# Attention scores in rounds of three tiles with three PSUM buffers, and one shared PSUM bank for all other matrix work

## The chip, the cores and the metric

The kernel runs on one core of a Trainium2 chip. The metric is the time of one execution on the device in microseconds (us); lower is better. The core has a matrix engine (PE, TensorE) that writes only to PSUM, a memory of eight banks with 512 fp32 columns on 128 partitions each; a vector engine (DVE, VectorE); an engine for functions such as the exponential (ACT, ScalarE); GpSimd (POOL) and SyncE (SP), which here issue DMA transfers.

## The reference

Two independent layers, whose outputs are concatenated. `A` is a long convolution over 2048 positions for 576 channels: a kernel K is generated from a state-space model, and y = irfft(rfft(u) * rfft(K)) + u * Dskip. `B` is attention with one shared key and value head:

```python
q = (x @ wq).reshape(B, S, H, Dh).transpose(0, 2, 1, 3)   # 32 heads of 18, S = 2048
k, v = x @ wk, x @ wv                                     # one head of 18
scores = einsum("bhqd,bkd->bhqk", q, k) * Dh ** -0.5
o = einsum("bhqk,bkd->bhqd", softmax(scores), v)
out_b = o.transpose(0, 2, 1, 3).reshape(B, S, 576) @ wo
```

Everything is fp32.

## The kernel before

**Attention** (class `Attention`). The 2048 queries are cut into four chunks `c` of 512, the heads into eight groups `g` of four, the keys into 16 blocks `kb` of 128. That gives 512 steps (line 587). In a step, `scores` (L350) is called for two pairs of heads: two matmuls with 55 rows each fill the two banks of one score tile `s` (128 keys x 2 heads x 512 queries), and one ScalarE instruction (L362) writes the exponentials to a tile `P` in SBUF. The 55 rows hold q and k split into a high and a low part, and a bound on the scores, so no row maximum is needed. The product (L628) of the step before then multiplies four heads of `P` by v, in four 32-column strips of the array, and adds up over the 16 blocks in the bank `ops`; a column of ones in v gives the softmax denominator. At the 16th block VectorE copies `ops` out (`gather`, L365) and SP stores it.

**Other matrix work**, called filler here, is put between scores and product. `qproj` (L271) makes the queries of seven heads and 512 positions, as two halves of 256 columns with five chunks of matmuls each; `queries` (L288) then splits them with three reads of the whole bank on VectorE, distributes the rows by DMAs of POOL, and makes the bound with a small matmul `up`. `outproj` and `outproj_part` (L408, L432) make the output `op` in pieces of 288 columns. The class `Conv` makes the convolution in twelve blocks of 48 channels: tables on VectorE and ScalarE, `kgen` (L887, tile `kg`), two forward transforms per block (`transform`, L930, tiles `lu`, `hu`, `lk`, `hk`), long VectorE arithmetic, and an inverse transform `iy` (L1018). Every one of them is a group of matmuls into a bank, followed by VectorE reading the bank out.

**PSUM** (lines 168 to 171): two score tiles of two banks, one bank `ops`, two banks `q` which q, op and up take in turn, one bank `m` for the convolution. Eight banks in all.

**The order** of PE, ScalarE and VectorE is that of the program text; PE works it off in that order. `main` (L578) decides it when the program is written out, with a model of the three engines' clocks (`Clock`). Generators (`Stream`) give their work piece by piece and say what the next piece needs: "p" is PE work that may start at a time `ready`, "v" is VectorE work, and a flag `holds` says that a group of matmuls is open. In each step, after the two scores, filler is taken as long as a credit lasts (about 0.56 us of PE time a step, from `TOTAL` and `LAST`), then comes the product. `q_free` and `Conv.free` are the model's times at which a bank is read out.

Of the kernel before, what the change touches and what calls it, by code (L numbers as in the profile page):

```python
# [31 lines left out]


RATE = 1.75
AHEAD = 0.8
# [17 lines left out]
class Clock:  # L53
# [6 lines left out]
    def __init__(self):  # L60
        self.t = self.v = self.a = 0.0
        self.work = 0.0
        self.s = [0.0, 0.0]
# [4 lines left out]
    def act(self, cost, after=0.0):  # L68
        self.a = max(self.a, after) + cost
        return self.a  # L70

# [36 lines left out]
class Stream:  # L108
# [18 lines left out]
    def go(self, step, credit):  # L127

        k = self.k
        if not self.live or self.kind == "b" or self.kind == "p" and (credit <= 0 or k.t < self.ready):  # L130
            return False
        if self.kind == "v" and (k.t < self.ready or k.v > k.t + self.ahead):
            return False
        if self.kind == "w":
            if self.asked == step:
                return False
            self.asked = step
        self.advance()
        return True
# [10 lines left out]
class Attention:  # L150
# [7 lines left out]
    def __init__(self, tc, ctx, aps, clock):  # L158
# [7 lines left out]
        self.pp = pool("a_p", 4)  # L166
        self.dr = pool("a_dr", 4, space=bass.MemoryType.DRAM)
        self.ps_s = pool("ps_s", 2, space=PSUM)
        self.ps_o = pool("ps_o", 1, space=PSUM)
        self.ps_q = pool("ps_q", 2, space=PSUM)  # L170
        self.ps_m = pool("ps_m", 1, space=PSUM)
# [9 lines left out]
    def setup(self, tp, conv):  # L181
# [8 lines left out]
        self.sel = cp.tile([P, 138], F32, name="sel_sb")  # L190
# [27 lines left out]
        nc.scalar.dma_start(self.sel, a["sel"])  # L218
# [6 lines left out]
        self.outs, self.step, self.due, self.q_free, self.scaled = [], 0, 1 << 30, [0.0, 0.0], {}  # L225
# [3 lines left out]
        kps = self.ps_q.tile([P, CT], F32, tag="q", name="kps")  # L229
        self.qps = self.ps_q.tile([P, CT], F32, tag="q", name="q0_0")  # L230
        pv = self.ps_m.tile([P, CT], F32, tag="m", name="vps")
        for k in range(5):
            for ps, j in ((kps, 0), (None, 0), (pv, 32)):
                if ps is None:
                    matmul4(nc, self.qps, self.wq[0][:, k, :], x0[:, k, :], start=(k == 0), stop=(k == 4))
                    continue
                for c in range(NCH):
                    nc.tensor.matmul(ps[32 * c:32 * c + 32, :], wkv[:, k, j:j + 32], xr[:, k, c - 1, :] if c else x0[:, k, :],
                                     start=(k == 0), stop=(k == 4), tile_position=(0, 32 * c))
        nc.scalar.activation(kh, kps, AF.Copy)  # L240
        V.tensor_reduce(km[:, 4:5], kps, axis=AX.X, op=ALU.max, apply_absolute_value=True)
        V.tensor_scalar(km[:, 0:4], self.sel[:, 134:138], km[:, 4:5], None, op0=ALU.mult)
# [12 lines left out]
        pk = self.ps_q.tile([P, 4], F32, tag="q", name="kmx")  # L255
        nc.tensor.matmul(pk[:126, :], self.sel[:, 8:134], km[:, 0:4], start=True, stop=True)
# [4 lines left out]
        vp = self.ps_m.tile([P, 4, P], F32, tag="m", name="vp")  # L261
# [9 lines left out]
    def qproj(self, c, m, xt):  # L271

        nc, V, K = self.nc, self.V, self.k
        m0, mn = MT[m]
        self.q_left = 10
        yield "p", max(self.q_free[0], K.t), False
        ps = self.ps_q.tile([P, CT], F32, tag="q", name=f"q{c}_{m}")
        for f in range(2):
            sl = slice(f * 256, f * 256 + 256)
            for k in range(5):  # L280
                matmul4(nc, ps[:, sl], self.wq[m][:, k, :], xt[:, k, sl], start=(k == 0), stop=(k == 4))
                K.pe(0.43)
                self.q_left -= 1
                if (f, k) != (1, 4):
                    yield "p", 0.0, True
        yield from self.queries(c, m, ps)

    def queries(self, c, m, ps):  # L288
# [3 lines left out]
        K.v = max(K.v, K.t)  # L292
        qh = self.p2.tile([P, CT], F32R, tag="qh", name=f"qh{c}_{m}", bufs=1)
        ql = self.p2.tile([P, CT], F32R, tag="ql", name=f"ql{c}_{m}", bufs=1)
        ab = self.p2.tile([P, 1], F32, tag="ab", name=f"ab{c}_{m}")
        if (c, m) == (0, 0):
            nc.scalar.activation(qh[:mn, :], ps[:mn, :], AF.Copy)
        else:
            V.tensor_copy(qh[:mn, :], ps[:mn, :])
            V.tensor_tensor(ql[:mn, :], ps[:mn, :], qh[:mn, :].bitcast(F32), op=ALU.subtract)  # L300
        V.tensor_reduce(ab[:mn, :], ps[:mn, :], axis=AX.X, op=ALU.max, apply_absolute_value=True)
        if (c, m) == (0, 0):
            V.tensor_tensor(ql[:mn, :], ps[:mn, :], qh[:mn, :].bitcast(F32), op=ALU.subtract)
# [22 lines left out]
        yield "p", max(K.v + 0.4, self.q_free[0]), False  # L326

        up = self.ps_q.tile([P, 8], F32, tag="q", name=f"up{c}_{m}")
# [5 lines left out]
        self.q_free = self.q_free[1:] + [K.v + 0.3]  # L334
# [15 lines left out]
    def scores(self, c, pr, kb):  # L350

        nc = self.nc
# [5 lines left out]
        K = self.k  # L358
        K.pe(0.335, K.s[pr % 2])
        K.s[pr % 2] = K.act(0.925, K.t + 0.27) + 0.1  # L360
# [4 lines left out]
    def gather(self, c, g, o_ps):  # L365
        nc = self.nc
        o_sb = self.p2.tile([P, CT], F32, tag="o", name=f"o{c}_{g}")
        self.k.v = max(self.k.v, self.k.t)
        self.V.tensor_copy(o_sb, o_ps)
        nc.sync.dma_start(self.od[c][g * P:(g + 1) * P, :], o_sb)  # L370
# [37 lines left out]
    def outproj(self, c):  # L408
        nc, V, K = self.nc, self.V, self.k
        o = self.oT  # L410
        self.o_left += 40
        yield "p", max(self.scaled[4], self.q_free[0]), False
        for t in range(4):
            ob = self.p1.tile([P, D], F32, tag="ob", name=f"ob{c}_{t}", bufs=2)
            for nh in range(2):
                ps = self.ps_q.tile([P, 288], F32, tag="q", name=f"op{c}_{t}_{nh}")
                for m, (m0, mn) in enumerate(MT):
                    matmul4(nc, ps, o[:mn, m, t * P:(t + 1) * P], self.wo[:mn, m, nh * 288:(nh + 1) * 288], start=(m == 0), stop=(m == 4))
                    K.pe(0.5)
# [4 lines left out]
                V.tensor_copy(ob[:, nh * 288:(nh + 1) * 288], ps)  # L424
                self.q_free = self.q_free[1:] + [K.v + 0.3]
                if nh == 0:
                    yield "p", self.q_free[0], False
            nc.sync.dma_start(self.a["outb"][c * CT + t * P:c * CT + (t + 1) * P, :], ob)
            if t < 3:
                yield "p", self.q_free[0], False  # L430

    def outproj_part(self, c, ms, part):  # L432
# [3 lines left out]
        self.o_left += 8 * len(ms)  # L436
        for t in range(4):
            for nh in range(2):
                yield "p", max(self.scaled[ms[-1]], self.q_free[0]), False
                ps = self.ps_q.tile([P, 288], F32, tag="q", name=f"op{c}_{t}_{nh}_{ms[0]}")  # L440
                cs = slice(nh * 288, (nh + 1) * 288)
                for m in ms:
                    matmul4(nc, ps, o[:126, m, t * P:(t + 1) * P], self.wo[:126, m, cs], start=(m == ms[0]), stop=(m == ms[-1]))
                    K.pe(0.5)
# [8 lines left out]
                self.q_free = self.q_free[1:] + [K.v + 0.3]  # L453

    def finish(self, c, part, o_ps, w4, b4):
# [3 lines left out]
        o_sb = self.p2.tile([P, CT], F32, tag="o", name="o_last")  # L459
        rc = self.p2.tile([P, CT], F32, tag="o", name="rc_last")  # L460
        half = [slice(f * 256, f * 256 + 256) for f in range(2)]
        cols = [slice(nh * 288, nh * 288 + 288) for nh in range(2)]
        bc = self.ps_m.tile([P, CT], F32, tag="m", name="bc")
# [14 lines left out]
        def invert(f):  # L478
            V.reciprocal(rc[:, half[f]], rc[:, half[f]])
            nc.tensor.matmul(bc[:, half[f]], b4, rc[:, half[f]], start=True, stop=True)  # L480

        def scale(f):
            V.tensor_tensor(o_sb[:, half[f]], o_sb[:, half[f]], bc[:, half[f]], op=ALU.mult)
        for nh in range(2):
            begin(0, nh, self.ps_q.tile([P, CT], F32, tag="q", name=f"fin0_{nh}"))
        for t in (1, 2):
# [18 lines left out]
        begin(3, 1, self.ps_q.tile([P, CT], F32, tag="q", name="fin3_1"))  # L505
# [6 lines left out]
    def side(self):  # L512
# [3 lines left out]
        yield from self.queries(0, 0, self.qps)  # L516
# [23 lines left out]
    def prepare(self):  # L540

        nc = self.nc
        while True:
# [11 lines left out]
            if ms[0] == 3:  # L555
                self.w4 = self.p1.tile([P, D], F32, tag="ob", name="w4", bufs=2)
# [21 lines left out]
    def main(self, conv, flag):  # L578
# [4 lines left out]
        K.t = K.v = K.a = conv.free = 0.0  # L583
        side.ready, self.q_free = 0.0, [0.0, 0.0]
        for st in conv.streams:
            st.ready = 0.0
        steps = [(c, g, kb) for c in range(NCH) for g in range(8) for kb in range(16)]
        prev, o_ps, credit, filled = None, None, 0.0, 0.0

        prep = Stream(self.prepare(), K, 99.0)  # L590

        def drain():
            while self.todo or self.busy or self.outs:
                if self.todo or self.busy:
                    prep.advance()
                if self.outs:
                    side.advance()
        for i, at in enumerate(steps + [None]):
            cur = None
            if at is not None:  # L600
                self.step = i
                c, g, kb = at
                if (g, kb) == (0, 0):
                    self.od[c] = self.dr.tile([8 * P, CT], F32, tag="od", name=f"od{c}")
                cur = [self.scores(c, 2 * g, kb), self.scores(c, 2 * g + 1, kb)]
                ready = K.act(0.0)
                credit = min(credit + min(max((TOTAL - filled) / max(LAST - i, 20), 0.45), 0.58 if i < 384 else 0.68), 0.75)
                nxt = (c, 2 * g + 3) if g < 7 else (c + 1, 1)
                more = True
                while more:  # L610
                    more, t = False, K.t

                    idle = max(K.s[0] - K.t - 0.96, K.s[1] - K.t - 1.3) - 0.15
# [568 lines left out]
```

## Time and profile before

| | |
|---|---|
| median of 3 runs | 1288.39 us (1286.58 to 1291.62) |
| the profiled execution | 1288.89 us, span of its instructions 1287.0 us |
| PE matmul records | 1223.3 us, 95% of the span |
| ScalarE | 1064.3 us, 83% |
| VectorE | 991.5 us, 77% |
| idle time of ScalarE ahead of exponentials, ended by PE's scores | 179.3 us |
| mean granted PE clock | 0.989 |

The span runs from the first to the last instruction. A group in the profile is a source line, an engine, an operation and its tiles, written out<-in; x is the count. "PEld" is the loading of weights into PE, which overlaps matmuls. In a timeline each row has its start, its duration, and in brackets how long the engine had been idle and what ended that. Rows of one kind that follow one another are merged with their count; an fp32 matmul of the program is two records (two passes), a score matmul is one.

### The profile page before, as it was taken

To read this page: it belongs to the slowest core of one execution; us is meant where nothing else is said; L and a number is where in the kernel's file an instruction comes from. 1 tells how busy PE (TensorE), PEld (TensorE's weight loads), DVE (VectorE), ACT (ScalarE), POOL (GpSimd) and SP (SyncE) were. 2 spreads that over 40 slices of the span, in tenths; PEclk is the share of its full clock that TensorE was granted. 3 is DMA by queue.
4 is the path that set the end of the run, shared out by engine and by line. 5 is a ranking of instruction groups with operands and counts; after the bars stand their busy time and mean duration, and the time that the engine had idled before them with its cause. 6 is when DMAs were issued, how large, how long until landed. Compare 5 with 4: busy or idle time off the path is not lost.

```text
span 1287.0 us, 32922 instructions
## 1 busy us (share of the span) xinstructions
PE 1223.3 (95%) x13762; PEld 472.4 (37%) x13762; DVE 991.5 (77%) x1612; ACT 1064.3 (83%) x1101; POOL 227.8 (18%) x450
## 2 busy tenths in 40 slices
PE   5999999899999999999999999999899999899997
PEld 1333343243334344343334334334233334334332
DVE  4778878878878968978977976976977987786842
ACT  2689989888988888888888888888988888788884
POOL 3342102203110110231312110221302120110000
PEclk9899999899999999999999999999999999899999
DMA  7621022121120112021122011312103112021011
GB/s 224 174 70 35 17 67 65 30 75 47 53 75 23 42 58 76 25 82 51 36 75 71 29 51 42 99 33 76 31 27 107 29 40 66 13 59 64 26 39 39
DMA packets 56779, 75.35 MB, mean 59 GB/s; under 512 B 19393, under 2 KB 30017, under 8 KB 56113
## 3 DMA queue, kind: packets, MB, share of 16 engines
q1 hardware_dynamic: 35784, 58.22, 13.8%
q0 software_dynamic: 20288, 14.39, 5.1%
q8 instruction: 110, 1.80, 0.6%
q10 hardware_dynamic: 552, 0.58, 0.1%
q14 instruction: 45, 0.36, 0.1%
HBM read 35.28 MB, written 22.54 MB: 45 GB/s over the span
## 4 chain that ended last, share of the span: by engine, by line
PE 67%; issue 12%; DVE 12%; ACT 6%; POOL 1%; DMA 1%; SPq 0%; DVEq 0%; ACTq 0%; POOLq 0%
PE ops L628 24%; PE s L357 21%; ACT P L362 6%; PE op L147 5%; PE q L147 4%; PE kg L898 3%; PE iy L147 2%; DVE ks L86 2%; DVE acc L86 2%; PE lu L147 1%; PE hu L147 1%; PE hk L147 1%; PE lk L147 1%; POOL aug L321 1%; DVE f L86 1%
## 5 line engine op out<-in xcount | busy, mean ns | idle before, releaser
L362 ACT ACTIVATE P<-s 128x1024 f32<-128x1024 f32 x1024 | 985.7, 1023 | 188.7 <-PE s L357 179.3
L628 PE MATMUL ops<-P,v_sb 128*32 128x512 f32 x4096 | 548.8, 601 | 4.9 <-DVE o L90 4.6
L357 PE MATMUL s<-aug,kaug 55*128 55x512 f32 x2048 | 432.5, 475 | 38.2 <-ACT P L362 35.1
L357 PEld LDWEIGHTS s<-aug,kaug 55*128 55x128 f32 x2048 | 186.2, 185 | 543.0 <-ACT P L362 523.8
L321 POOL DMA_DIRECT2D aug<-qh x252 | 127.0, 520 | 769.0 <-DVE qh L90 394.3
L628 PEld LDWEIGHTS ops<-P,v_sb 128*32 128x32 f32 x4096 | 116.9, 110 | 90.8 <-issue 35.1
L147 PE MATMUL q<-x,wq_sb 128*32 128x256 f32 (+2 forms) x1480 | 105.9, 396 | 0.0
L147 PE MATMUL op<-wo_sb,oT 126*32 126x288 f32 (+1 forms) x1152 | 94.8, 414 | 0.0
L90 DVE COPY ksb<-kg 128x192 f32<-128x192 f32 x48 | 17.6, 366 | 83.3 <-PE kg L898 83.3
L321 POOL DMA_DIRECT2D aug<-ql x128 | 65.0, 523 | 8.4 <-issue 5.4
L86 DVE TENSOR_TENSOR tab<-tab,tt 128x576 f32<-128x576 f32 (+1 forms) x72 | 59.2, 822 | 1.8
L147 PEld LDWEIGHTS q<-x,wq_sb 128*32 128x32 f32 (+1 forms) x1480 | 42.5, 109 | 47.6 <-issue 26.3
L86 DVE TENSOR_TENSOR tab<-tab 128x576 f32<-128x576 f32 (+1 forms) x72 | 59.0, 819 | 1.0
L347 POOL DMA_DIRECT2D aug<-sh x61 | 35.2, 586 | 134.0 <-DVE sh L94 133.7
L86 DVE TENSOR_TENSOR tab<-sum,r 128x576 f32<-128x576 f32 (+1 forms) x72 | 58.9, 818 | 0.0
L86 DVE TENSOR_TENSOR tt<-f,sum 128x576 f32<-128x576 f32 (+1 forms) x72 | 58.8, 817 | 0.0
L86 DVE TENSOR_TENSOR tab<-r,dif 128x576 f32<-128x576 f32 (+1 forms) x72 | 58.8, 817 | 0.0
L86 DVE TENSOR_TENSOR sck<-lk,sck 128x384 f32<-128x384 f32 x48 | 24.5, 553 | 31.7 <-PE lk L147 31.7
L86 DVE TENSOR_TENSOR acc<-acc,pt 128x1728 f32<-128x1728 f32 (+2 forms) x36 | 48.7, 1353 | 0.2
L86 DVE TENSOR_TENSOR pt<-us,ks 128x1728 f32<-128x1728 f32 (+2 forms) x36 | 48.7, 1352 | 0.1
L86 DVE TENSOR_TENSOR u<-u,iy 128x384 f32<-128x384 f32 x24 | 13.3, 554 | 38.3 <-PE iy L147 38.3
L898 PE MATMUL kg<-tab 128*32 128x64 f32 x2304 | 42.1, 221 | 0.4 <-DVE tab L86 0.4
(118 smaller groups left out, 1003.7 us busy)
## 6 DMA issues: line engine op xcount, KB each, us to landing
aug<-qh POOLq DMA_DIRECT2D x252, 36.0 KB, 1.9
od<-o SPq DMA_DIRECT2D x31, 256.0 KB
aug<-ql POOLq DMA_DIRECT2D x128, 36.0 KB, 2.0
u<-u SPq DMA_DIRECT2D x12, 384.0 KB
kd<-ksb SPq DMA_DIRECT2D x12, 384.0 KB
kt<-kd SPq DMA_DIRECT2D x48, 96.0 KB
outa<-u SPq DMA_DIRECT2D x12, 384.0 KB
oT<-od SPq DMA_DIRECT2D x16, 252.0 KB
```

The lines of the kernel that those rows point to most:

```text
L86: return self.v.tensor_tensor(out, *a, **k)
L90: return self.v.tensor_copy(out, *a, **k)
L147: nc.tensor.matmul(ps[j:e], w[:, j:e], x, start=start, stop=stop, tile_position=(0, j))
L321: q.dma_start(t[b:b + 18, :], src[r:r + 18, :])
L347: nc.gpsimd.dma_start(self.aug[(c, h // 2)][54:119:64, :], sh)
L357: nc.tensor.matmul(ps[:, j, :], self.kaug[r, kb * P:(kb + 1) * P], t[r, :], start=True, stop=True)
L362: nc.scalar.activation(pt, ps, AF.Exp, scale=SCALE)
L628: nc.tensor.matmul(o_ps[32 * j:32 * j + 32, :], self.v[:, pk, :], pts[j // 2][:, j % 2, :], start=(pk == 0), stop=(pk == 15), tile_positio ...
L898: nc.tensor.matmul(ps[32 * g:32 * g + 32, d, :], t[:, :32], t[:, 32:], start=(j == 0), stop=(j == 1), tile_position=(0, 32 * g))
```

## The change

- There are three score tiles (`NS` = 3), six banks. A round computes three of them, that is three pairs of heads, one after the other, then the three exponentials; products of the rounds before follow, each when its two `P` tiles are there. There are six `P` buffers instead of four.
- One bank `fb` of two halves of 256 columns takes all other matrix work, in turn (`half`). The model keeps two times `fill` at which the halves are read out; a group may start at `fill[0]`, the older one.
- To fit a half, groups get smaller. A transform makes four groups of 192 columns where it made two of 384, each with its own reads by VectorE; `iy` likewise; `op` is made in three pieces of 192 columns instead of two of 288; each half of `q` is read out by itself.
- Only one group of matmuls may be open at a time (`lock`, `holder`).
- `o` and `ob` have one buffer instead of two. The setup uses score buffers, `ops` and `fb` for its own matmuls, and loads `sel` in two parts.

The core of the diff, lines left out:

```diff
+NS = 3
+NP = 6
...
+    def filled(self, least=0.0):
+        self.fill = self.fill[1:] + [max(self.v, least) + 0.3]
...
-        self.ps_s = pool("ps_s", 2, space=PSUM)
+        self.ps_s = pool("ps_s", NS, space=PSUM)
         self.ps_o = pool("ps_o", 1, space=PSUM)
-        self.ps_q = pool("ps_q", 2, space=PSUM)
-        self.ps_m = pool("ps_m", 1, space=PSUM)
+        self.fb = pool("ps_f", 1, space=PSUM).tile([P, 2, 256], F32, name="fill")
+        self.turn = 0
...
+    def half(self, n):
+        self.turn ^= 1
+        return self.fb[:, self.turn, :n]
...
         for f in range(2):
             sl = slice(f * 256, f * 256 + 256)
+            yield "p", K.fill[0], False
+            ps = self.half(256)
             for k in range(5):
-                matmul4(nc, ps[:, sl], self.wq[m][:, k, :], xt[:, k, sl], start=(k == 0), stop=(k == 4))
+                matmul4(nc, ps, self.wq[m][:, k, :], xt[:, k, sl], start=(k == 0), stop=(k == 4))
...
+            V.tensor_copy(qh[:mn, sl], ps[:mn, :])
+            V.tensor_tensor(ql[:mn, sl], ps[:mn, :], qh[:mn, sl].bitcast(F32), op=ALU.subtract)
+            V.tensor_reduce(ab[:mn, f:f + 1], ps[:mn, :], axis=AX.X, op=ALU.max, apply_absolute_value=True)
+            K.filled()
...
         for j in range(2):
-            for half in (1, 0):
-                yield "p", max(ready, self.free), False
...
+            for r in (2, 0, 3, 1):
+                yield "p", max(ready, K.fill[0]), False
+                q = 4 * j + r
+                ps = self.half(NE)
+                matmul4(nc, ps, self.dft[:, q * P:(q + 1) * P], src(r))
+                K.pe(0.33)
                 self.evacuate()
-                if half:
+                if r >= 2:
                     V.tensor_copy(x, ps)
                 else:
-                    V.tensor_tensor(ac[:, 2 * j:2 * j + 2, :], ps, x, op=ALU.add)
-                    V.tensor_tensor(bd[:, 0:4:3, :] if j == 0 else bd[:, 1:3, :], ps, x, op=ALU.subtract)
+                    V.tensor_tensor(ac[:, 2 * j + r, :], ps, x, op=ALU.add)
+                    V.tensor_tensor(bd[:, ((0, 3), (1, 2))[j][r], :], ps, x, op=ALU.subtract)
                 self.evacuated()
...
+        for r in range(0, len(pairs), NS):
+            new = range(r, min(r + NS, len(pairs)))
...
+                ss[i] = self.scores(i, c, 2 * g + j, kb, 0.335 if i == r else 0.215)
+            K.t += 0.11
+            for i in new:
+                while (i - NP) // 2 >= behind:
+                    product(behind)
+                    behind += 1
...
+                pts[i] = self.exponentials(i, c, 2 * g + j, kb, *ss[i])
+                done[i] = K.a
+            s = self.step
+            state["credit"] = min(state["credit"] + NS / 2 * min(max((TOTAL - state["filled"]) / max(LAST - s, 20), 0.45), 0.58 if s < 384 else 0.68), 1.2)
...
+            while behind < r // 2:
+                fill(free() - 0.96 * (r // 2 - behind))
+                product(behind)
+                behind += 1
+            fill(free())
```

`fill` takes pieces from the streams while the credit is over 0.3, or while the model has PE idle before `then`; `free` is the model's time at which ScalarE has left the buffers of the next round.

333 lines of the change are left out of this document (175 added, 158 removed).

## The prediction

> **What bounds the kernel now.** I read the page's engine lines and costliest groups first. In a group the number after the bar is busy time, then the mean of one in ns, then the idle time before it with its releaser.
>
> ```profile
> PE 1223.3 (95%) x13762; PEld 472.4 (37%) x13762; DVE 991.5 (77%) x1612; ACT 1064.3 (83%) x1101; POOL 227.8 (18%) x450
> PE 67%; issue 12%; DVE 12%; ACT 6%; POOL 1%; DMA 1%; SPq 0%; DVEq 0%; ACTq 0%; POOLq 0%
> L362 ACT ACTIVATE P<-s 128x1024 f32<-128x1024 f32 x1024 | 985.7, 1023 | 188.7 <-PE s L357 179.3
> L628 PE MATMUL ops<-P,v_sb 128*32 128x512 f32 x4096 | 548.8, 601 | 4.9 <-DVE o L90 4.6
> L357 PE MATMUL s<-aug,kaug 55*128 55x512 f32 x2048 | 432.5, 475 | 38.2 <-ACT P L362 35.1
> L357 PEld LDWEIGHTS s<-aug,kaug 55*128 55x128 f32 x2048 | 186.2, 185 | 543.0 <-ACT P L362 523.8
> ```
>
> PE is on 67% of the chain that ended last, but its 95% is an upper figure: the matmul records overlap, so I count from starts. The timeline of an ordinary stretch shows what one step costs (two score tiles, some filler, one product):
>
> ```profile
> 700.79 0.79 PE L357 MATMUL s<-aug,kaug 55*128 55x512 f32 x4
> 701.40 1.94 ACT L362 ACTIVATE P<-s 128x1024 f32<-128x1024 f32 x2 [0.37 <-PE s L357]
> 701.51 0.86 PE L147 MATMUL hk<-kt,dft_sb 128*32 128x192 f32 x16
> 702.18 1.04 PE L628 MATMUL ops<-P,v_sb 128*32 128x512 f32 x8
> 702.43 0.56 DVE L90 COPY sck<-hk 128x384 f32<-128x384 f32 x1 [1.34 <-PE hk L147]
> 703.15 0.73 PE L357 MATMUL s<-aug,kaug 55*128 55x512 f32 x4
> 703.81 0.86 PE L147 MATMUL lk<-kt,dft_sb 128*32 128x192 f32 x16
> ```
>
> From start to start: scores 0.66 (703.15 to 703.81), filler 0.67, product 0.97 (702.18 to 703.15). How long the main stretch is comes from the views of the tiles s and P; after min/median/max in ns stand the first and the last start in us:
>
> ```profile
> L357 PE MATMUL s<-aug,kaug x2048: 383/493/792, 33.0 to 1267.4; 55*128 55x512 f32 x187
> L628 PE MATMUL ops<-P,v_sb x4096: 589/592/1061, 38.3 to 1270.0; 128*32 128x512 f32 x196
> ```
>
> So 512 steps lie between 33.0 and about 1269.7, 1236.6 us, or 2.415 us a step. PE's own need is 512 x (0.66 + 0.97) = 835 us, and the filler 286 (the planner's TOTAL, line 36; its 0.66 for a pair of transform chunks agrees with the 0.67 above). That is 1121: **some 116 us of the main stretch are waits of PE**. ScalarE needs less: four exponentials in a row last 3.77 (below), so they follow one another every (3.77 - 1.02) / 3 = 0.917 us, 939 for 1024, and 1064.3 - 985.7 = 79 of other work: 1018 us. Neither engine is full; each waits for the other, since two score buffers leave little room:
>
> ```profile
> 1262.93 0.91 PE L357 MATMUL s<-aug,kaug 55*128 55x512 f32 x4
> 1263.34 0.18 PEld L357 LDWEIGHTS s<-aug,kaug 55*128 55x128 f32 x2 [0.23 <-ACT P L362]
> 1263.52 3.77 ACT L362 ACTIVATE P<-s 128x1024 f32<-128x1024 f32 x4 [0.23 <-PE s L357]
> 1264.76 0.49 PE L357 MATMUL s<-aug,kaug 55*128 55x512 f32 x2
> 1265.51 0.19 PEld L357 LDWEIGHTS s<-aug,kaug 55*128 55x128 f32 x2 [0.57 <-ACT P L362]
> 1266.93 0.91 PE L357 MATMUL s<-aug,kaug 55*128 55x512 f32 x4
> ```
>
> Two steps without filler take 4.00 us here although PE needs 2 x 1.63 = 3.26: the second score tile waits for ScalarE to leave its buffer. With filler (the stretch at 701) ScalarE waits 0.37 a pair instead.
>
> **The change, part by part.**
>
> *Rounds of three tiles: PE saves 57 us.* Bursts of scores fall from 512 to 342. A third tile in a burst appears nowhere in this trace. It costs no less than its weight load (185 ns above) and no more than half a burst of two (0.33); I take 0.22, near the load, since the ends of 0.66 also hold the change to and from the other matmul shape. A round is then 0.66 + 0.22 = 0.88 against 1.5 x 0.66 = 0.99: 0.11 x 341 = 38 us (48 by the lower end, 0 by the upper). Second, the product: its eight records last 1.04 together and 592 ns each, so its two passes start 0.45 - 0.02 = 0.43 apart, 0.86 for both, and 0.11 of the 0.97 goes into turning to scores. That is paid once a round: 170 x 0.11 = 19 us (0 if each product pays it anyway). New need of PE: 1121 - 57 = 1064 us.
>
> *A third score buffer, six P buffers and products that come a round behind their scores* let ScalarE run ahead. Of the 116 us of waits I keep 38 (ScalarE's twelve excursions to other tables, the o_ps bank that is still one buffer, the start) and let 78 go; the bounds are 0 and 116. What is late next is PE itself.
>
> *One bank for all other TensorE work.* Today q, op and up turn in two banks of their own and the convolution has a third. The change puts them in two halves of one bank, in smaller groups: 192 transform groups (96 before), 48 iy (24), 48 kg, 38 q (19), 19 up, 72 op (48), 417 in all against 254. The planner lets a group start when the half used two groups back is read out. But this trace shows that two engines are kept apart by the bank, even where no data forces it:
>
> ```profile
> 24.31 0.60 ACT L240 ACTIVATE kh<-kps 128x512 fp32r<-128x512 f32 x1 [5.80 <-PE kps L238]
> 24.94 0.69 DVE L98 TENSOR_REDUCE km<-kps 128x1 f32<-128x512 f32 x1 [3.57 <-ACT kh L240]
> 1272.75 0.36 DVE L491 TENSOR_SCALAR rc_last<-ops 128x256 f32<-128x256 f32 x1
> 1273.14 0.38 ACT L492 ACTIVATE o_last<-ops 128x256 f32<-128x256 f32 x1 [1.68 <-DVE rc_last L491]
> ```
>
> km reads kps and not kh, o_last reads ops and not rc_last: both pairs are two reads of one bank, and still the second starts 0.03 us after the first ends. I take it that a matmul into one half waits likewise for VectorE's read of the other half. Two reads of the same columns do not prove that, so it stays a rival (C).
>
> The Trainium skill, "PSUM — Partial Sum Buffer", section "PSUM bank collisions raise a hardware error", says that any two engines on one bank and 32-partition quadrant at once are an error whether or not the columns meet, so that accesses have to be ordered by bank. By that rule the 152 us below belong in the sum, by the planner's two halves they don't; the trace agrees as far as reads go, and no run so far has a matmul beside a read of the other half.
>
> What one such turn costs follows from these rows (evacuations, and one hand-over from VectorE to PE):
>
> ```profile
> L90 DVE COPY ksb<-kg 128x192 f32<-128x192 f32 x48 | 17.6, 366 | 83.3 <-PE kg L898 83.3
> L90 DVE CAST qh<-q 126x512 fp32r<-126x512 f32 x15 | 10.3, 687 | 15.1 <-PE q L147 15.1
> L90 DVE COPY ob<-op 128x288 f32<-128x288 f32 x24 | 10.9, 452 | 2.9 <-PE op L147 2.9
> L86 DVE TENSOR_TENSOR sck<-lk,sck 128x384 f32<-128x384 f32 x48 | 24.5, 553 | 31.7 <-PE lk L147 31.7
> 1274.15 0.42 DVE L483 TENSOR_TENSOR o_last<-o_last,bc 128x256 f32<-128x256 f32 x1 [1.04 <-PE bc L480]
> 1274.63 0.64 PEld L147 LDWEIGHTS fin<-w,o_last 128*32 128x32 f32 x16 [0.92 <-DVE o_last L483]
> ```
>
> VectorE starts 0.25 after PE could have gone on (702.18 to 702.43), reads 192 columns in 0.37, and PE loads again 0.06 later: 0.68, say 0.7 where the next group stands directly behind. After a low transform group with two subtractions or sums it is 1.0, after a q half with three reads of 256 columns (each near 0.42, between 0.366 and 0.452) 1.6. Where a product (0.97) or scores lie between, 0.7 is covered. Queued behind the waiting matmul are all scores and products, since PE keeps its order; ScalarE then waits for them.
>
> How often? The filler budget is 286 / 341 = 0.84 us a round, spent greedily in the round's first call; chunks are 0.33 to 0.43, 742 of them by the code's loops, 2.2 a round. One of these follows a product or scores, 1.2 follow another chunk: 55%. Of 417 group starts 229 would stand directly behind another group; the planner itself bars a third short group in a call, so I take 190 (bounds: 60, if q and op, which go on over rounds, mostly end with a call; 260). At 0.8 on average: **190 x 0.8 = 152 us** (48 to 208).
>
> *VectorE* pays for smaller pieces: a transform's six reads of 384 columns (6 x 0.553 = 3.3) become twelve of 192 (4.4), 24 x 1.1 = 26 us; q three of 0.68 become six of 0.42 and one tiny, 12; op 72 x 0.37 for 48 x 0.45, 5; iy 4. These 47 us raise 991.5 to 1038 of 1287, beside PE's work; without that cover they would come on top. *The rest:* ob and o lose their second buffer, so a copy waits for the store before it, but op's next write to ob comes rounds later and o's every eight steps; SP's and POOL's queues get no new transfer but one split load of sel; the setup uses other banks for the same work. I cost these at 0, between -1 and +3 (a store that holds up a copy at the end, or a setup step that finds its bank taken).
>
> **The sum**, against the profiled execution (span 1287.0, its own time 1288.9, so 1.9 lie around it; the median shown, 1288.39, is 0.5 below): 1287.0 - 57 - 78 + 152 = 1304 span, with VectorE's and the rest's 0, and 1.9 around it: **1306 us**.
>
> **Rivals.**
>
> *B, few turns are exposed.* The bank is ordered, but groups seldom stand back to back, or VectorE's read ends under a wait for ScalarE. For it: the row of ksb, where VectorE is idle ahead of all 48 reads and so reads at once. Against it: the greedy first call. With 105 turns of 0.8 the sum is 1287 - 57 - 78 + 84 + 2 = 1238. Below 160 exposed turns the change gains over half a per cent.
>
> *C, the halves are independent* for TensorE and VectorE, as the planner has it: no turn costs, 1287 - 135 + 2 = 1154, and as ScalarE's 1018 then stand close behind PE's 1064 and each will hold up the other some 25 us more, 1180. Against it speak the two ordered pairs above.
>
> *E, VectorE is late at the turn.* Slower than forecast and on the far side of before:
>
> ```profile
> DVE qh L90 <- PE q L147: 19.8, 6, 6.0
> DVE ob L90 <- PE op L147: 2.9, 4, 1.3
> ```
>
> These rows of the waits (total, times, longest) say that VectorE waited for PE in 6 of 19 q groups and 4 of 24 op copies: in the others it was still at older work, which today a second bank covers. If half of the 110 q and op groups find 0.8 of such work, 44 us are added: 1350. It decides once over 30 groups are late beside the 190 turns. Against it: a slower PE gives VectorE time.
>
> *D, nothing to see:* turns eat just what rounds give, about 135 us or 160 to 176 turns: 1282 to 1295.
>
> **Numbers.** A measurement of this kernel tells about 0.5% (6.4 us) from no change. Forecast A (1295 to 1330) 0.40, E (over 1330) 0.13, D 0.10, B (1200 to 1281) 0.33, C 0.04. Faster by over 0.5%: B and C, 0.37; the same: D, 0.10; slower: A and E, 0.53. The range leaves out C, B's lowest and E's highest part: 1218 to 1355.
>
> **What would show it.** Right: PE waits for VectorE's reads of the fill tile (sck, scu, ksb, u, ob, ql or ab as releasers ahead of L147 or L898) summing to 100 us and more, where now there are hardly any; scores in bursts of six matmuls with 0.88 from the first to the next other matmul; ScalarE's idle time behind PE at or above 179.3 us. Wrong: such waits under 80 us, or matmuls into the fill bank while VectorE reads it (C); a burst of 0.99 (no saving by rounds); PE waiting for P as much as before (no gain by the third buffer).

## The result and the profile after

The changed kernel takes **1446.68 us** (median of four runs, 1445.57 to 1449.61) where the kernel before took 1290.01 on the same chip: **a ratio of 1.122, 95% interval 1.119 to 1.125**. The forecast, 1306, is 141 us short, and the time lies outside its range.

The page of the kernel after, with the rows that answer to those of before (scores are now L387, exponentials L395, products L658):

```profile
PE 1199.9 (83%) x14338; PEld 479.2 (33%) x14338; DVE 1031.4 (71%) x1880; ACT 1048.5 (73%) x1101; POOL 225.3 (16%) x450
PE 61%; DVE 25%; ACT 6%; issue 5%; DMA 2%; SPq 1%; POOL 1%; DVEq 0%; ACTq 0%
L395 ACT ACTIVATE P<-s 128x1024 f32<-128x1024 f32 x1024 | 969.8, 1030 | 342.0 <-PE s L387 314.2
L658 PE MATMUL ops<-P,v_sb 128*32 128x512 f32 x4096 | 546.9, 606 | 5.0 <-DVE o L99 5.0
L387 PE MATMUL s<-aug,kaug 55*128 55x512 f32 x2048 | 363.4, 444 | 36.4 <-ACT P L395 34.0
```

VectorE has gone from 12% to 25% of the chain, and ScalarE sits idle for 314.2 us until PE has scores for it (179.3 before). What PE waits for stands in the groups of the filler, by engine and line (after the second bar the idle time ahead, with its releasers):

```profile
L156 PE MATMUL fill<-x,wq_sb 128*32 128x256 f32 (+2 forms) x1440 | 103.9, 398 | 31.8 <-DVE ab L107 12.6 <-DVE scu L95 6.9 <-DVE sck L95 4.5
L156 PE MATMUL fill<-wo_sb,oT 126*32 126x192 f32 (+1 forms) x1728 | 94.9, 331 | 38.2 <-DVE ob L99 9.5 <-DVE part L95 7.3 <-DVE ab L107 6.7
L156 PE MATMUL fill<-kt,dft_sb 128*32 128x192 f32 x768 | 51.3, 339 | 34.1 <-DVE sck L99 18.8 <-DVE sck L95 6.8 <-DVE ab L107 4.8
L156 PE MATMUL fill<-u,dft_sb 128*32 128x192 f32 x768 | 50.9, 337 | 33.9 <-DVE scu L99 16.6 <-DVE scu L95 11.3 <-DVE ab L107 2.7
L156 PE MATMUL fill<-w,dft_sb 128*32 128x192 f32 x768 | 46.0, 348 | 25.4 <-DVE u L95 13.5 <-DVE w L95 9.7 <-DVE ab L107 1.8
L970 PE MATMUL fill<-tab 128*32 128x64 f32 x2304 | 41.7, 220 | 11.6 <-DVE ksb L99 5.8 <-DVE ab L107 2.7 <-DVE ob L99 1.9
```

Together PE stood 175 us ahead of these groups, nearly always for a read by VectorE; 9.7 us are one wait near the end for `w`, a result that VectorE writes. (With the small group of `up` it is the 182 us of the table below.) An ordinary stretch of the timeline shows one round with two turns:

```profile
703.09 0.96 PE L387 MATMUL s<-aug,kaug 55*128 55x512 f32 x6
703.69 2.86 ACT L395 ACTIVATE P<-s 128x1024 f32<-128x1024 f32 x3 [0.22 <-PE s L387]
703.99 0.53 PE L156 MATMUL fill<-kt,dft_sb 128*32 128x192 f32 x8
704.77 0.35 DVE L99 COPY sck<-fill 128x192 f32<-128x192 f32 x1
705.17 0.53 PE L156 MATMUL fill<-kt,dft_sb 128*32 128x192 f32 x8 [0.66 <-DVE sck L99]
705.77 0.62 DVE L95 TENSOR_TENSOR sck<-fill,sck 128x192 f32<-128x192 f32 x2 [0.66 <-PE fill L156]
706.45 0.64 PE L156 MATMUL fill<-x,wq_sb 128*32 128x256 f32 x8 [0.74 <-DVE sck L95]
706.91 1.04 PE L658 MATMUL ops<-P,v_sb 128*32 128x512 f32 x8
```

The burst of three lasts 0.90 (703.09 to 703.99), as forecast. But three groups follow one another, and each start but the first waits until VectorE has read the group before it, although that lies in the other half. Where the time lies along the run shows in the view of the tiles P and ops (first and last start); the first row is the kernel before, the others the kernel after:

```profile
L362 ACT ACTIVATE P<-s x1024: 1015/1023/1061, 34.1 to 1268.5; 128x1024 f32<-128x1024 f32 x171
```
```profile
L395 ACT ACTIVATE P<-s x1024: 1014/1025/1077, 44.9 to 1406.0; 128x1024 f32<-128x1024 f32 x171
L658 PE MATMUL ops<-P,v_sb x4096: 590/592/1062, 51.1 to 1407.5; 128*32 128x512 f32 x196
```

From the first exponential to the start of the last product (the **stretch**) it is 1235.9 us before and 1362.6 after, 126.7 more; the start takes 10.8 more; from the last product to the end of the span (the **end**) it is 17.0 before and 1443.8 - 1407.5 = 36.3 after, 19.3 more.

### The profile page after: what moved, and what is told of

Same layout as the page of the kernel before. It is cut to its first block, busy times and chain, and to the rows that moved or that the text cites. A ratio compares the mean times of both kernels' runs of the same rounds, so it can differ in the third digit from the quotient of the medians.

```text
span 1443.8 us, 34389 instructions
## 1 busy us (share of the span) xinstructions
PE 1199.9 (83%) x14338; PEld 479.2 (33%) x14338; DVE 1031.4 (71%) x1880; ACT 1048.5 (73%) x1101; POOL 225.3 (16%) x450
## 4 chain that ended last, share of the span: by engine, by line
PE 61%; DVE 25%; ACT 6%; issue 5%; DMA 2%; SPq 1%; POOL 1%; DVEq 0%; ACTq 0%
PE ops L658 24%; PE fill L156 17%; PE s L387 16%; ACT P L395 6%; DVE tab L95 2%; PE fill L970 2%; DVE ks L95 2%; DVE acc L95 2%; DVE f L95 2%; DVE us L95 1%; DMA xr<-xT 1%; DVE scu L95 1%; DVE u L95 1%; DVE r L95 1%; DVE pt L95 1%
## 5 line engine op out<-in xcount | busy, mean ns | idle before, releaser
L395 ACT ACTIVATE P<-s 128x1024 f32<-128x1024 f32 x1024 | 969.8, 1030 | 342.0 <-PE s L387 314.2
L658 PE MATMUL ops<-P,v_sb 128*32 128x512 f32 x4096 | 546.9, 606 | 5.0 <-DVE o L99 5.0
L387 PE MATMUL s<-aug,kaug 55*128 55x512 f32 x2048 | 363.4, 444 | 36.4 <-ACT P L395 34.0
L387 PEld LDWEIGHTS s<-aug,kaug 55*128 55x128 f32 x2048 | 173.4, 188 | 351.8 <-ACT P L395 261.3
L658 PEld LDWEIGHTS ops<-P,v_sb 128*32 128x32 f32 x4096 | 112.2, 110 | 121.9 <-issue 89.9
L156 PE MATMUL fill<-x,wq_sb 128*32 128x256 f32 (+2 forms) x1440 | 103.9, 398 | 31.8 <-DVE ab L107 12.6
L156 PE MATMUL fill<-wo_sb,oT 126*32 126x192 f32 (+1 forms) x1728 | 94.9, 331 | 38.2 <-DVE ob L99 9.5
L156 PEld LDWEIGHTS fill<-wo_sb,oT 126*32 126x32 f32 (+1 forms) x1728 | 47.8, 109 | 97.8 <-issue 30.5
L156 PE MATMUL fill<-kt,dft_sb 128*32 128x192 f32 x768 | 51.3, 339 | 34.1 <-DVE sck L99 18.8
L156 PE MATMUL fill<-u,dft_sb 128*32 128x192 f32 x768 | 50.9, 337 | 33.9 <-DVE scu L99 16.6
L156 PEld LDWEIGHTS fill<-x,wq_sb 128*32 128x32 f32 (+2 forms) x1440 | 42.9, 111 | 91.0 <-issue 29.3
L156 PE MATMUL fill<-w,dft_sb 128*32 128x192 f32 x768 | 46.0, 348 | 25.4 <-DVE u L95 13.5
L99 DVE COPY ksb<-fill 128x192 f32<-128x192 f32 x48 | 17.3, 361 | 62.7 <-PE fill L970 62.5
L95 DVE TENSOR_TENSOR sck<-fill,sck 128x192 f32<-128x192 f32 x96 | 29.8, 352 | 37.9 <-PE fill L156 37.9
```

Source lines behind the costliest of these rows:

```text
L95: return self.v.tensor_tensor(out, *a, **k)
L99: return self.v.tensor_copy(out, *a, **k)
L156: nc.tensor.matmul(ps[j:e], w[:, j:e], x, start=start, stop=stop, tile_position=(0, j))
L387: nc.tensor.matmul(ps[:, j, :], self.kaug[r, kb * P:(kb + 1) * P], t[r, :], start=True, stop=True)
L395: nc.scalar.activation(pt, ps, AF.Exp, scale=SCALE)
L658: nc.tensor.matmul(o_ps[32 * j:32 * j + 32, :], self.v[:, kb, :], pts[2 * n + j // 2][:, j % 2, :], start=(kb == 0), stop=(kb == 15), tile ...
```

## Experiments

The theory: program order lets a matmul into `fill` wait for VectorE's read of the last group, and that is most of the loss. The rival: the new order of work, its small groups and VectorE's added reads cost by themselves, and the waits are a symptom. One table of all runs first, in us. Idle is PE's idle time ahead of all groups of filler; the span is the profiled execution's, times are medians.

| run | time | first exponential | stretch | end | idle |
|---|---|---|---|---|---|
| before | 1288.4 to 1290.0 | 34.1 | 1235.9 | 17.0 | 2 |
| after | 1446.7 | 44.9 | 1362.6 | 36.3 | 182 |
| e1 planner knows | 1465.3 | 45.6 | 1262.1 | 156.8 | 133 |
| e2 one half | 1449.7 | 44.3 | 1363.5 | 36.1 | 183 |
| e3 rounds of two, one bank | 1493.6 | 45.6 | 1428.0 | 16.6 | 155 |
| e4 rounds of two, two banks of a tile | 1495.0 | 45.9 | 1427.1 | 17.4 | 155 |
| e5 rounds of two, two tiles | 1318.2 | 44.9 | 1255.2 | 17.1 | 14 |
| e6 five P, opened early | 1509.5 | 34.3 | 1388.6 | 85.5 | 200 |
| e7 reads elsewhere | 1251.2 | 44.9 | 1174.8 | 29.6 | 7 |
| e8 whole bank, planner knows | 1384.7 | 44.9 | 1259.6 | 77.1 | 92 |
| e9 VectorE further ahead | 1498.1 | 44.6 | 1434.8 | 18.0 | 202 |
| e10 as e5, large groups, early P | 1310.5 | 35.0 | 1257.8 | 17.3 | 8 |
| e11 as e7, rounds of two | 1239.7 | 45.3 | 1175.6 | 17.1 | 0 |
| e12 as e8, rounds of two | 1316.3 | 44.8 | 1233.6 | 34.4 | 47 |
| e13 as e12, five P, early | 1313.2 | 34.6 | 1240.7 | 34.9 | 50 |
| e14 as e13, faster convolution | 1317.2 | 34.7 | 1257.1 | 19.9 | 40 |
| e15 as e13, other settings | 1312.2 | 35.8 | 1256.2 | 18.8 | 57 |
| e16 as e13, less margin | 1337.4 | 34.3 | 1283.2 | 18.7 | 66 |

**e1: let the planner know.**

```diff
-        self.fill = self.fill[1:] + [max(self.v, least) + 0.3]
+        self.fill = [max(self.v, least) + 0.3] * 2
```


> Edit: the model lets a filler group start only once the group just before it has been read out, instead of the one before that; the single bank and the rounds of three stay. Theory T (a matmul into one half of the bank waits for VectorE's read of the other half): PE's idle time ahead of filler groups, 175 us in the changed kernel, falls below 70 us, since other work now lies between a group and the next, and the time falls from 1446.7 to about 1340 us (1290 to 1390). Rival R (the halves are independent, and the time is lost by smaller groups and by the new order): groups are held back for nothing, 1440 us or more.

The stretch fell by 100 us, but the time rose to 1465 (ratio 1.138, 1.135 to 1.141). Inside the stretch PE's idle time ahead of filler fell from 170 us to 54, below the 70 that theory T expected. But the planner put less filler into the stretch: a sixth of `op` (288 of 1728 matmul records) and parts of two blocks of the convolution were left over. Behind the last product PE stands idle another 79 us ahead of them, at a granted clock of 0.50 to 0.61 of full speed (0.97 over most of the stretch). The waits of ScalarE show it, two parts of the last evacuation, one of them held up 140.7 us behind that work:

```profile
ACT o_last L525 <- DVE rc_last L524: 142.4, 2, 140.7
```

So the forecast of 1340 failed, and the time of this run doesn't decide by itself: what is saved in one place is paid in another.

**e2: is the second half of any use?**

```diff
-        return self.fb[:, self.turn, :n]
+        return self.fb[:, 0, :n]
```


> Edit: every filler group uses the same half of the bank; the order of the program is unchanged. Theory T: the second half was never of use, so the time stays at 1446.7 us within 1%. Rival R: groups that could overlap the read of the other half now cannot, so PE waits more and the time rises by 60 us or more.

1449.7 against 1446.7, with 183 us of idle time against 182: nothing is lost by taking the second half away. It never let two groups overlap.

**e3, e4, e5: bank or tile?** Three kernels with the same instructions in the same order: rounds of two (`NS` = 2), which frees two banks, and groups as small as after. One of the two serves the setup and the last matmuls in all three; that edit is left out below. In e3 the two places are halves of one bank, in e4 two banks of one tile, in e5 two tiles of one bank each.

```diff
-        self.fb = pool("ps_f", 1, space=PSUM).tile([P, 2, 256], F32, name="fill")
+        self.fb = pool("ps_f", 1, space=PSUM).tile([P, 2, CT], F32, name="fill")   # e3, e4
+        self.fb = [fp.tile([P, CT], F32, name=f"fill{j}") for j in range(2)]       # e5
...
+        return self.fb[:, 0, self.turn * 256:self.turn * 256 + n]                  # e3
+        return self.fb[:, self.turn, :n]                                           # e4
+        return self.fb[self.turn][:, :n]                                           # e5
```


> Edit: rounds of two score tiles with two score buffers; filler in two halves of one bank as in the changed kernel. Theory T: PE still waits at turns, 1400 us or more (up to 1480). Rival R: with rounds as before the change the time goes back to about 1300 us (1270 to 1330).

> Edit: as the run with two tiles and one bank, with the same order of the program, but the two halves lie in two banks. Theory T: the waits at turns go, PE's idle time ahead of filler falls from over 150 us to under 40, and the time is 100 to 200 us below that run, near 1290 us (1250 to 1330). Rival R: the same as that run within 1%.

> Same instructions in the same order as the two kernels before with rounds of two and a fill tile of two banks (1493.6 and 1495.0 us), but the two places are now two tiles of one bank each. Theory W (the time goes into waits that are ordered by the tile: a matmul waits for VectorE's read of the group before it, wherever that lies): PE's idle time ahead of filler falls from about 151 us to under 50, and the time by 100 to 200 us, to 1300 to 1395. Theory O (the order of work, its small groups and VectorE's added reads are what costs): the waits at turns are only a symptom, the time stays above 1450.

e3 came out 14 us above its range (1400 to 1480). e4 equals e3 within 0.1%; the expectation for it was wrong. Its timeline shows matmuls that wait for a read of the other bank:

```profile
699.82 0.53 PE L156 MATMUL fill<-kt,dft_sb 128*32 128x192 f32 x8
700.42 0.62 DVE L95 TENSOR_TENSOR sck<-fill,sck 128x192 f32<-128x192 f32 x2 [0.66 <-PE fill L156]
701.10 0.53 PE L156 MATMUL fill<-kt,dft_sb 128*32 128x192 f32 x8 [0.74 <-DVE sck L95]
```

e5, with two tiles, is 177 us faster than e4 (1495.0 to 1318.2), and the same group of matmuls waits for next to nothing (e4 first, then e5):

```profile
L156 PE MATMUL fill<-kt,dft_sb 128*32 128x192 f32 x768 | 51.4, 339 | 36.3 <-DVE sck L95 16.1 <-DVE sck L99 9.3 <-DVE ob L99 5.4
```
```profile
L156 PE MATMUL fill<-kt,dft_sb 128*32 128x192 f32 x768 | 44.5, 332 | 0.3 <-DVE sck L95 0.3
```

So the program orders accesses by the **tile**: in e3 and e4 PE stands idle ahead of the same 193 filler matmuls. No run here has two tiles in one bank, so whether PE could write one half of a bank while VectorE reads the other stays open.

**e7: the same without turns.** All matmuls of the kernel after stay, and all reads by VectorE, but the reads take an SBUF tile of the same size; the filler's results are left unused.

```diff
                 self.evacuate()
+                ps = self.zz(NE)        # columns of dft_sb; likewise in iy, kg, op, up; of the x tile in q
                 if r >= 2:
                     V.tensor_copy(x, ps)
```


> The kernel after, but VectorE's reads of the groups of filler (transforms, iy, kg, q, op, up) take a tile in SBUF of the same size in place of the fill tile; all matmuls and all reads stay, so that neither engine waits for the other at a turn. This leaves the results of the filler unused. Theory W (turns are what costs): PE's idle time ahead of filler under 15 us (175 in the kernel after), the main stretch falls from 1362 us by 150 to 215 us to between 1147 and 1212, the time to 1230 to 1300. Theory O (order, small groups, VectorE's added work): PE then waits elsewhere, the time stays above 1400.

The group of the k transforms, and the tiles P and ops, in this kernel:

```profile
L156 PE MATMUL fill<-kt,dft_sb 128*32 128x192 f32 x768 | 43.9, 334 | 0.0
```
```profile
L397 ACT ACTIVATE P<-s x1024: 1012/1028/1103, 44.9 to 1218.1; 128x1024 f32<-128x1024 f32 x171
L662 PE MATMUL ops<-P,v_sb x4096: 590/592/1062, 51.0 to 1219.7; 128*32 128x512 f32 x196
```

PE waits nowhere ahead of this filler, and the stretch is 1174.8. The time is 1251.2 us, ratio to before 0.971 (0.968 to 0.974). Without its turns the kernel after would thus be at most some 38 us faster than the one before, and **its turns cost 195**: 188 in the stretch and 7 at the end. Both kernels give PE the same work in the same order. Set side by side, the steps from one filler matmul to the next take 210 us more in the kernel after, and all other steps together 14 less. e7 changes two things besides PE's waits: VectorE goes on without PE's results, and its copies of 192 columns take 0.26 us from SBUF where they take 0.36 from `fill`. So 195 is an upper figure for PE's own waits; e5, where every result is used, gains 177 on e4. The rival falls; small groups and VectorE's work are not the cause (e10 against e5 says the same: large groups leave the stretch at 1258 against 1255, though by e13 below the early start of e10 puts some 7 us more into it).

**e11: why does the third buffer give so little?** In the kernel without turns the stretch is only 61 us shorter than before, where the forecast had 135. I measured bursts from their first start to the next other matmul, those with all their records, from 50 us to shortly before the end. They last 0.830 on average before (501 bursts, 0.662 when free), 1.121 in e7 (337, 0.892 when free) and 1.085 after (338). The excess is 86 us before (512 x 0.168), 78 in e7 (342 x 0.229), 66 after. e11 is e7 with rounds of two:

```diff
-        for r in range(0, len(pairs), NS):
-            new = range(r, min(r + NS, len(pairs)))
+        for r in range(0, len(pairs), 2):
+            new = range(r, r + 2)
```


> The kernel with VectorE's reads elsewhere (1251.2 us; it has no waits at turns, and leaves the filler's results unused) with its three score buffers, but rounds of two tiles. In the earlier one the bursts of three last 78 us more in all than free bursts would (mean 1.121 us against 0.892), nearly the 86 of before, so the third buffer saved PE hardly any waiting. Theory R (a round takes all three buffers at once, so PE still waits until ScalarE has left the last of them): with one buffer more than a round needs, the excess of the bursts falls below 30 us; PE's own need rises by some 60 for the added bursts and changes of shape, and the time is 1240 to 1265. Rival (ScalarE's pace is what holds PE up, whatever the buffers): the excess stays above 60 and the time is 1280 to 1320.

The waits of PE's weight loads for a score buffer, with total, times and longest, in e7 and then in e11:

```profile
PEld s L389 <- ACT P L397: 349.9, 471, 7.4
```
```profile
PEld s L389 <- ACT P L397: 26.1, 8, 8.2
```

471 waits become 8, and a burst lasts 0.707 (0.662 when free): 23 us of excess. **A round that takes all the buffers has no buffer to spare**; it waits until ScalarE has left the last one. The price of rounds of two is what rounds of three saved, so the stretch stays (1175.6 against 1174.8); the 12 us that e11 is faster lie at the end, which puts its time just below its range.

**e8, e12: the best use of one bank.** Groups as large as before, each with the whole bank, with the planner of e1; e12 adds rounds of two.

```diff
+        return self.fb[:, :n]          # fb of 512 columns; transform, iy, op, q as before
```


> The kernel after with the group sizes of before (384, 288 and 512 columns; 254 groups instead of 417), each with the whole fill bank, and a planner that lets a group start only when its model has the read of the last one done. Rounds of three stay. Theory W: PE's idle time ahead of filler under 70 us (175 after), main stretch 1215 to 1260 us (1362 after); the last block of the convolution is then partly left for the end, 20 to 60 us behind the last product: 1285 to 1350. Theory O (small groups alone are not the cause, the order is): above 1400.

> The kernel with whole-bank groups and a planner that knows of the wait (1384.7 us), again with three score buffers, but rounds of two. Theory R: PE's waits inside bursts fall, a group of filler finds a burst and a product between itself and the next more often (512 rounds, not 342), so that PE's idle time ahead of filler falls from 87 us to under 60: main stretch 1220 to 1250 us (1259.5 in the earlier one), time 1300 to 1360. Rival: nothing gained by the order, 1375 or above.

e8 missed its range by 35 us: the end took 77 us, not 20 to 60, and 92 us of idle time stayed where under 70 were expected, 56 of them in the stretch. e12 came out in its range: stretch 1233.6, shorter than before by 2, but 10 us more at the start and 17 at the end.

**e6, e9, e13 to e16: start and end.** The P buffers after lie on memory of the setup. The first exponential waits for the last of its loads; after first, then e13, with P opened ahead of the setup:

```profile
44.91 1.94 ACT L395 ACTIVATE P<-s 128x1024 f32<-128x1024 f32 x2 [19.10 <-DMA kaug<-kl]
```
```profile
34.58 1.94 ACT L392 ACTIVATE P<-s 128x1024 f32<-128x1024 f32 x2 [9.16 <-PE s L384]
```
```diff
+            at.open(ctx)               # e6, e10, e13 to e16: ahead of the setup's pool
             with tc.tile_pool(name="setup", bufs=1) as tp:
...
-NP = 6
+NP = 5
```


> The kernel after, with the P buffers opened ahead of the setup's memory as in the kernel before, and five of them instead of six, since six do not fit. Theory S (the first exponential waits until every load of the setup has been used, because its buffer lies on the setup's memory): first exponential near 34 us instead of 44.9, and the time 11 us lower, 1433 to 1440, if the sixth buffer is worth nothing. Rival: the sixth buffer matters as much as the start, 1444 to 1455.

The start came back as expected, but in rounds of three five buffers also change the order of products and filler: 26 us more in the stretch, 49 more at the end. The time, 1509.5, lies above both expected ranges.

```diff
-AHEAD = 0.8
+AHEAD = 1.6                            # e9
```


> The kernel after, with VectorE's work of the convolution allowed 1.6 us ahead of PE in the planner's model instead of 0.8. The last inverse transforms then come before score tile 1020 of 1024, where in the kernel after the last ones come behind all of them. Theory L (the longer end is the convolution's last block, drained alone behind the attention): from the last product to the end about 16 us instead of 36, the time near 1425 to 1432, if the main stretch stays. Rival: the same work then stands in the main stretch, with the same turns, and the time stays within 1440 to 1455.

The end fell to 18.0, near the 16 of theory L, but the stretch rose by 72, and 1498.1 lies above both expected ranges: more changed than the place of the last inverse transforms, and what it was is not shown. With rounds of two the number of P buffers leaves the order alone:

```diff
-RATE = 1.75                            # e14
-PACE = 1.68
+RATE = 2.1
+PACE = 1.9
...
-AHEAD = 0.8                             # e15, with up to 0.66 us of filler a step
+AHEAD = 1.2
...
-        self.fill = [max(self.v, least) + 0.3] * 2
+        self.fill = [max(self.v, least)] * 2      # e16
```


> The kernel with whole-bank groups, three score buffers and rounds of two (1316.3 us), with five P buffers opened ahead of the setup's memory instead of six behind it. Theory S (the first exponential waits for the setup's loads since its buffer lies on their memory): first exponential near 34.5 us instead of 44.8, everything else as it was, 1304 to 1309. Rival: the fifth or sixth buffer is worth as much, 1313 to 1325.

> The same with the convolution's pace in the planner raised (PACE 1.9, RATE 2.1 instead of 1.68 and 1.75), so that its last inverse transforms come ahead of score tile 992 of 1024 and nothing of it is left for the end. Theory L: from the last product to the end 15 to 19 us instead of 34, main stretch as it was or up to 8 us longer: 1286 to 1300. Rival: the moved work costs its turns in the main stretch, as with VectorE further ahead: 1306 or above.

> The same as the kernel with the early start, with the last inverse transforms ahead of score tile 1004 by other settings (VectorE 1.2 us ahead, up to 0.66 us of filler a step). Theory L: the end as short, 15 to 19 us, 1286 to 1300. Rival: 1306 or above.

> The same as the kernel with the early start, but the planner takes the bank for free as soon as its model has VectorE's read done, without 0.3 us more. The last inverse transforms come ahead of score tile 1010. If 0.3 us is what a turn really takes beyond the read, PE's idle time ahead of filler rises by up to 254 x 0.3 = 76 us less what products cover: time 1300 to 1340 although the end is shorter. If the margin was too large, 1280 to 1295.

e13 starts 10.2 us earlier and ends 3 us earlier: 7 of the 10 come back in the stretch, and 1313.2 lies at the edge of its rival's range, not in that of theory S. e14 and e15 shorten the end by 15 and 16, and the stretch grows by as much. The rivals of both (1306 or above) were right: **time at the start and the end is mostly work that otherwise stands in the stretch**, not a term of its own. e16 shows that the planner's 0.3 us are needed (24 us slower).

**e10**, two tiles, large groups, early P:

> The kernel of the experiment with two fill tiles of one bank each (1318.2 us), with the group sizes of before (384, 288, 512 columns) and P buffers opened ahead of the setup. Theory: small groups cost little beside PE, the start costs 11: first exponential near 34 us, main stretch 1235 to 1255 us as in the earlier kernel (1255) or before (1236), time 1285 to 1308. Rival: small groups cost what VectorE's added reads take, some 40 us: the main stretch falls to 1215 and the time to 1265 to 1275, faster than before.

1310.5 us, just above its range, ratio 1.016 (1.015 to 1.018). No version that computes everything beat the kernel before; this one and e15 (1312.2) come nearest. Why the stretch of e10 is still 22 us longer than before, with only 8 us of idle time ahead of filler, is not shown; it has two tiles for filler where the kernel before has three banks, and only one group may be open at a time.

## Why the prediction was wrong

The direction was right (slower, 0.53), and so was the mechanism that it put first. But the direction was partly luck: the forecast's 17 us are the difference of -135 and +152, which a modest error in either term turns round. The time lies above 1330, where only rival E (0.13) was. Term by term, in the stretch and against the profiled execution:

- **Rounds of three, -57: right.** A free burst of three lasts 0.892 against 0.88 forecast: 512 x 0.662 - 342 x 0.892 = 34 us saved, where 38 were meant. From the last pass of a product to scores PE takes 0.11 more than from pass to pass, and that step is recorded 289 times after against 510 before: 24 us, where 19 were meant.
- **Waits of PE, -78: the step that failed.** It kept 38 of 116 us of waits and let 78 go, since a third buffer lets ScalarE run ahead. The excess of the bursts went from 86 us to 66 after and 78 in e7: only 8 to 20 us went. The 58 to 70 us that stayed are about half of what the forecast is short. The buffer is there, but a round takes all three; e11 gives one to spare, and then 55 of the 78 go. The sign named for this case in the prediction, PE waiting for P as much as before, stands in the page: 34.0 us ahead of scores against 35.1 (55.6 in e7).
- **Turns, +152: right in kind, too small.** The count was good: 218 waits of PE for VectorE ahead of filler against 190. Set beside e7 step by step, the 211 of them that follow another filler matmul are of two kinds. In 147 VectorE begins to read at most 0.45 us after the last matmul of the group has started. These cost 0.80 on average, as forecast (0.66 with one read, 0.92 with two, 1.56 with three, where 0.7, 1.0 and 1.6 were meant). In the other 64 it begins later, in 59 of them straight from older work, and these cost 1.35. Its lateness adds up to 40 us: **rival E's mechanism came on top of the forecast's**, though not at q, where E put it (4 of the 64), but at the transforms (29), at `op` (16) and elsewhere. By e7 all turns together cost 195, since the other steps give 14 back. In one late turn of the kernel after, VectorE's own arithmetic (`f`) stands ahead of the read:
```profile
328.82 1.45 DVE L95 TENSOR_TENSOR f<-f,r 128x1248 f32<-128x1248 f32 x1
329.04 0.53 PE L156 MATMUL fill<-u,dft_sb 128*32 128x192 f32 x8
330.19 0.35 DVE L99 COPY scu<-fill 128x192 f32<-128x192 f32 x1
330.60 0.53 PE L156 MATMUL fill<-u,dft_sb 128*32 128x192 f32 x8 [1.02 <-DVE scu L99]
```

- **By the bank: wrong in its reason.** The two rows of reads from `kps` and `ops` were two reads of one tile as well, and could not tell bank from tile. The rule of the Trainium skill, "PSUM — Partial Sum Buffer", section "PSUM bank collisions raise a hardware error", asks for order by bank. The trace after agrees as far as it goes (705.17 and 706.45 above: both groups start behind the read of the other half), but e4 shows that this program orders two banks of one tile just as strictly (1495.0 against 1493.6), so order by bank is not what makes PE wait there.
- **VectorE at nothing: right.** It is busy 40 us more (47 forecast), and e5 against e10 shows that this is hidden beside PE. Its lateness at the turn is a different thing, the 40 us above; the row `ab` (31 us) is mostly q's three reads, some 1.2 us together each time, and not lateness.
- **The rest at nothing: wrong by 30 us** at first sight, 10.8 at the start and 19.3 at the end, since the P buffers moved behind the setup and the last inverse transforms behind the last scores. e13 to e15 show that most of this is work that would else stand in the stretch.

The sum by what was measured: 1287.0 - 58 (rounds) - 8 (waits) + 188 (turns) + 11 + 19 = 1439, against a span of 1443.8; some 5 us are not assigned.

Rival C, halves that are independent, was given 1180. The kernel without turns takes 1251: even with the mechanism away the gain was over-rated, and by the same term.

## What to carry to other kernels

Ask of each buffer how many of it one round takes: with as many buffers as a burst takes, the burst still waits for the last reader, and a further buffer saves waits only with one to spare. Two places in one PSUM tile are no double buffer, not even in two banks; give each its own tile, and let the planner's model wait for what the program waits for, but count what it then leaves for the end (157 us in e1). A saving at the start or the end counts only if the work moved out of there does not come back in the stretch.

## What was not expected of the hardware and its program

- Two banks of one tile are ordered like one: 1493.6 and 1495.0 us, and 1318.2 with two tiles, instruction for instruction the same work.
- A turn from PE to VectorE and back costs 1.2 to 1.3 us from start to start of two short groups (703.99 to 705.17 and 705.17 to 706.45 above), for a group that PE does in 0.33: the read itself is 0.35 to 0.62 of it.
- Leaving out all waits at turns while keeping every matmul, read and exponential makes the kernel 13.5% faster (1446.7 to 1251.2) although VectorE and PE are busy nearly as long: 992.0 and 1156.6 us against 1031.4 and 1199.9.
